# Sliding-window attention feeding a gated feed-forward block: transposes of queries and keys on TensorE in place of DMA, and a later place for the softmax sums

## Chip, cores and metric

The kernel runs on one core of one Trainium2 chip. The metric is the device time of one execution in microseconds (us). A core has TensorE (PE, matmuls into PSUM), VectorE (DVE), ScalarE (ACT), GpSimd (POOL) and SyncE (SP), which run side by side and wait for each other by semaphores; SP, ACT and POOL also issue DMA transfers, which 16 DMA engines carry out.

## What is computed

Attention with 8 batches, 8 heads, 576 positions and head size 64. Each query sees itself and the 127 positions before it; the score is lowered by a slope per head times the distance. Then a gated feed-forward block on all 4608 tokens (512 wide, 1536 hidden).

```python
scores = scale * np.matmul(q, k.transpose(0, 1, 3, 2))
mask = (rel >= 0) & (rel < window)                  # window = 128
scores = np.where(mask, scores + bias[None], -1000000000.0)
attn = np.exp(scores - max);  attn = attn / (sum(attn) + 1e-09)
attn_out = np.matmul(attn, v)                        # (8, 8, 576, 64)
x = attn_out.transpose(0, 2, 1, 3).reshape(4608, 512)
out = (gelu(x @ w_gate) * (x @ w_val)) @ w_out       # (4608, 512)
```

## The kernel before, in words

The feed-forward block works through nine groups g of 512 tokens, the attention through eight batches b of 576 tokens; results of the attention go into a ring `xT` (features on partitions, 3072 tokens), from which the groups read. The order of all engines is the order in which the program is written; nothing is rescheduled. While group g is worked on, batches g+1 and g+2 of the attention are slipped in between (line 915, `steps`, and the loop from line 933).

**A group.** `gate_val(g, f)` (line 615) runs for f = 0 to 11: eight matmuls of 512 columns (four with `wg`, four with `wv`, line 632), then Gelu on ACT (line 639) and a multiplication on DVE (line 640) into `hid`. `out_part(g, n)` (line 662) does n of the group's 16 output parts, three matmuls each (line 669); every fourth part is copied from PSUM by DVE or ACT (line 674, chosen by `by_dve`, line 651) and later stored by an SP DMA (`store`, line 657, called ahead of the next parts).

**A batch.** Queries and keys are loaded by POOL DMAs, cast to bf16, into `qs` and `ks` (token rows on partitions; two buffers, by b % 2), v into `vb`. `transposes_dma` (line 173) has SP issue six DMA transposes per batch that write `qT` and `kT` with the head dimension on partitions. Batches 0 and 1 have transposes of their own on TensorE (lines 784, 797 and 154). Scores are 64x64-weight matmuls: `scores` (line 235, batches 1 and 2) or `scores2` (line 267, from batch 3). Exponentials run on ACT (line 229), the decay with distance is multiplied in by DVE (line 232).

In `scores2` and in `products` two halves of the array write one PSUM bank, so the second half must come after the first: `relay` (line 208) puts a no-op on another engine's queue, SP by default, which waits for the first half's last matmul and on which the second half's first matmul waits.

**Sums from batch 3 on.** `add` (line 378) folds the overlapping blocks of probabilities into `T` (DVE, lines 385 to 394). `sums4` (line 426) sums `T` over partitions with 32 small matmuls (line 437) and takes reciprocals on DVE (line 442). `gather` (line 446) writes them to a DRAM buffer `rd` with two DMAs from ACT's queue, `spread_dma` (line 454) reads them back with two DMAs, repeated over 64 partitions each, into `rb`. `values` (line 547) runs the products with v (line 501) and multiplies them by `rb` into `xT` (DVE, line 565).

The written order for groups 2 to 5, b = g+2: gate steps f = 0 to 11, with the sums of batch b-1 after f = 3 (4 in group 2), its gather after 5 (6) and its spread after 7 (8); then 4 output parts, products of batch b-1, 4 parts, first scores of b and its additions, 4 parts, second scores of b and its additions, 4 parts. `load_qk(g+3)` and `load_v(g+2)` are issued by POOL at f = 9, behind a small copy (`mark`) that waits for that gate step. The DMA transposes of batch g+2 are issued at the start of group g.

Group g+1 reads the last 512 - 64(g+1) of its tokens from batch g+1, so its first gate matmuls need the scaled products of that batch.

`bank()` hands out PSUM banks, eight in all; a bank is free again when its last reader has run.

Of the kernel before, what the change touches and what calls it, by code (L numbers as in the profile page):

```python
# [8 lines left out]
BF16 = mybir.dt.bfloat16  # L9
# [23 lines left out]
def kernel(  # L33
# [10 lines left out]
    nc = tc.nc  # L44
    B, H, S, D = q.shape
# [22 lines left out]
    def bank():  # L68
        return psum.tile([128, 512], FP32, name="ps")
# [11 lines left out]
    ident = consts.tile([128, 128], BF16, name="ident")  # L81
# [11 lines left out]
    mark = consts.tile([1, 2], BF16, name="mark")  # L93
    last = consts.tile([128, DM], FP32, name="last")
# [7 lines left out]
    def rows(j):  # L102
        return 64 if j == 4 else 128
# [12 lines left out]
    def load_qk(b):  # L116
        load(qs[b % 2], q, b)
        load(ks[b % 2], k, b)

    def load_v(b, js=range(5)):  # L120
        load(vb[b % 2], v, b, js, 64)
# [48 lines left out]
        for n, lo in ((0, 0), (1, 384)):  # L170
            untangle(copy, b, n, what, c, c + 1, ps[:, lo:576])

    def transposes_dma(b):
        def of_k():
            nc.sync.dma_start_transpose(
                out=kT[b % 2].rearrange("p c (j t) -> p (c j) t", t=128),
                in_=ks[b % 2].rearrange("p j x -> p (j x)"))

        if b > 3:
            of_k()  # L180
        for j in range(5):
            nc.sync.dma_start_transpose(
                out=qT[b % 2][:, :, 128 * j:128 * j + 128], in_=qs[b % 2][:, j, :])
        if b <= 3:
            of_k()


    Ps = [consts.tile([128, H, 896], BF16, name=f"P{i}") for i in range(2)]
# [4 lines left out]


    def keys(b, c, m):
        if b < 2:
            return kT[b][:, c, 64 * m:64 * m + 64]
        at = 512 * (m // 2) + 128 * c + 64 * (m % 2)
        return kT[b % 2].rearrange("p c x -> p (c x)")[:, at:at + 64]

# [7 lines left out]
    def relay(mm, engine=nc.sync):  # L208
        by = engine.nop()
        depends(by, mm)  # L210
        return by
# [52 lines left out]

    def scores2(b, c0):
# [24 lines left out]
        todo.sort(key=lambda t: t[0])  # L292
        count, by = {c: 0 for c in pairs}, {}
        total = sum(len(parts_of(x, True)) for x in (0, 1))
        for _, i, c, both, x, m, q0, w, col in todo:
            half = slice(64 * i, 64 * i + 64)
            ps, col = (shared[c], col + 256 * i) if both else (own[c, i], col)
            mm = nc.tensor.matmul(  # L298
                out=ps[64 * x:64 * x + 64, col:col + w], lhsT=keys(b, c, m)[half, :],
                rhs=qT[b % 2][half, c, q0:q0 + w], start=True, stop=True)  # L300
            if both and i == 0:
                count[c] += 1
                if count[c] == total:
                    by[c] = relay(mm)
# [92 lines left out]
    sumrow, recip = {}, {}  # L397
# [45 lines left out]

    flat = {}

    def gather(b):
        flat[b] = d_pool.tile([H, S], FP32, name="rd")
        for s in (0, 1):
            lo, w = shape(b, s)
            nc.scalar.dma_start(  # L450
                out=flat[b][:, lo:lo + 2 * w].rearrange("h (x t) -> x h t", x=2),
                in_=sumrow[b][0:128:8, lo:lo + w])

    def spread_dma(b):
        for i in (0, 1):
            nc.scalar.dma_start(
                out=recip[b][64 * i:64 * i + 64, :, :],
                in_=flat[b][i:H:2, :].unsqueeze(0).to_broadcast((64, 4, S)))

# [153 lines left out]
    hid = {}  # L613
# [34 lines left out]
    acc = {}  # L648


    by_dve = {0: (0,), 1: (0, 1)}

# [245 lines left out]

    nc.gpsimd.memset(T[64:128, :, 0:64], 0.0)
    nc.gpsimd.memset(Ps[1][:, :, 0:64], 0.0)
    for t in (qs[0], ks[0]):
        nc.gpsimd.memset(t[64:128, 4, :], 0.0)
    load_qk(2)


    acts = (act, act, act, act)
    scales = []
    todo = {  # L910
        0: [("table",), ("s", 1, 0, (0, 1)), ("o", 0, 0, 0), ("o", 0, 1, 0), ("s", 1, 0, (2, 3)), ("o", 0, 0, 1), ("s", 1, 1, (0, 1)), ("o", 0, 1, 1), ("s", 1, 1, (2, 3), masks), ("pv+", 1, 0), 4, ("transposes", 2), ("pv+", 1, 1), 4],
        1: [("table",), ("s", 2, 0, (0, 1)), 3, ("s", 2, 0, (2, 3)), 2, ("s", 2, 1, (0, 1)), 2, ("s", 2, 1, (2, 3), masks), ("pv+", 2, 0, scales), 1, ("scale",), 2, ("pv+", 2, 1), 1, 2, ("s2", 3, 0), ("add", 3, 0), 3, ("s2", 3, 2), ("add", 3, 2, None, (0,))],
    }

    def steps(g):
        b = g + 2
        if g in todo:
            return todo[g]
        if b > B:
            return [16] if g < NG - 1 else [12, ("last", g)]  # L920
        if b == B:
            return [4, ("pv", b - 1), 12]
        return [("table",), 4, ("pv", b - 1), 4, ("s2", b, 0), ("add", b, 0), 4, ("s2", b, 2),
                ("add", b, 2), 4]


    def exp_table():
        nc.scalar.preload_act_table_set("natural_log_exp_and_others")

    RUN = {"s": scores, "s2": scores2, "add": add, "sum4": sums4, "gather": gather, "spread": spread_dma, "pv": values, "pv+": values_and_sums,  # L930
           "masks": flush, "table": exp_table, "transposes": transposes_dma, "last": out_last, "scale": lambda: scales.pop()(), "o": out_half}

    for g in range(NG):
        if 1 <= g < B - 2:
            transposes_dma(3 if g == 1 else g + 2)
        if g == 1:

            nc.gpsimd.tensor_copy(out=mark, in_=kT[1][0:1, 0, 512:514])
            load_qk(4)
            load_v(3)  # L940
        for f in range(9 if g == 0 else 0, NF):
            gate_val(g, f)
            if g == 2 and f == 2:
                add(3, 2, act, (1,))
            if g == 0 and f == 10:
                masks_of_last_blocks(0, 8)
            if g == 0 and f == 9:
                for c in range(4):
                    for w in (0, 1):
                        transpose(1, w, c, (act, dve)[w])  # L950
            if 2 <= g < B - 1:
                if f == (4 if g == 2 else 3):
                    sums4(g + 1)
                if f == (6 if g == 2 else 5):
                    gather(g + 1)
                if f == (8 if g == 2 else 7):
                    spread_dma(g + 1)
                if f == 9 and g + 2 < B:

                    nc.gpsimd.tensor_copy(out=mark, in_=hid[g][0:1, f, 0:2])  # L960
                    if g + 3 < B:
                        load_qk(g + 3)
                    load_v(g + 2)
        if g == 0:
            nc.gpsimd.memset(Ps[0][:, :, 0:64], 0.0)
            for t in (qs[1], ks[1]):
                nc.gpsimd.memset(t[64:128, 4, :], 0.0)
        for item in steps(g):
            if isinstance(item, int):
                out_part(g, item)  # L970
            else:
                RUN[item[0]](*item[1:])
        store()
        if g == 0:

            nc.gpsimd.tensor_copy(out=mark, in_=qT[0][0:1, 0, 512:514])
            load_qk(3)
            load_v(2)

# [29 lines left out]
```

## Time and profile before

| | |
|---|---|
| median of 3 runs | 338.54 us (338.36 to 339.22) |
| the profiled execution | 337.69 us |
| its span, first to last instruction | 335.9 us |
| TensorE granted clock | 1.000 |
| line 632, gate and value matmuls, PE busy | 223.4 us |
| line 669, output matmuls, PE busy | 87.6 us |
| line 501, products and some sums | 5% of the chain that ended last |
| DMA transposes | 36 issued by SP (30 of queries, 6 of keys) |

A row of the profile page's groups gives line, engine, operation, `out<-in` by the program's names, shapes and count, then busy time, mean nanoseconds of one instruction, and how long the engine was idle ahead of it and on what. Matmuls are pipelined, so the mean of one (379 ns for 512 columns) is longer than the distance between two starts. The chain of work that ended last is followed back from the last instruction: what it names is what the end was waiting for. Times inside the profile count from the start of the span.

### The profile page before, as it was taken

What the parts mean: (1) busy time and instruction counts of PE and PEld (TensorE: products, weight loads), DVE (VectorE), ACT (ScalarE), POOL (GpSimd) and SP (SyncE); (2) the same over time, 40 slices, a digit from 0 to 9 for tenths busy, and PEclk for the clock granted to TensorE, in tenths of its full rate; (3) what the DMA queues carried; (4) which work ended last, traced back from release to release, by engine and by line L of the source; (5) the groups of instructions that cost most, each with busy time, mean ns of one, the idle gap of its engine ahead of it and who ended that gap; (6) DMA issues with size and microseconds to landing.
All of it is one profiled execution on the core that took longest, in us unless ns stands there. A gap on an engine that the chain in (4) does not pass through costs nothing.

```text
span 335.9 us, 8087 instructions
## 1 busy us (share of the span) xinstructions
PE 327.7 (98%) x3273; PEld 169.5 (50%) x3316; DVE 192.9 (57%) x356; ACT 170.3 (51%) x318; POOL 108.3 (32%) x144
## 2 busy tenths in 40 slices
PE   8999999999999999999999999999999999999996
PEld 6667556444554454445544554445444544444444
DVE  7888776445779458845693469546964324303320
ACT  8974687438796339332943275335732233223322
POOL 6974784481193293009400860050000000000000
PEclk9999999999999999999999999999999999999999
DMA  8999999999999899969975999394105110020002
GB/s 216 170 197 191 205 164 189 117 181 137 183 161 153 181 184 198 164 161 134 184 163 104 153 187 179 81 166 83 64 3 140 64 65 0 1 96 31 0 31 96
DMA packets 149914, 43.49 MB, mean 129 GB/s; under 512 B 133588, under 2 KB 142836, under 8 KB 149876
## 3 DMA queue, kind: packets, MB, share of 16 engines
q0 software_dynamic: 107456, 18.10, 70.5%
q1 hardware_dynamic: 39104, 18.62, 25.4%
q10 hardware_dynamic: 3316, 6.25, 7.8%
q8 instruction: 26, 0.43, 0.5%
q14 instruction: 12, 0.10, 0.1%
HBM read 43.65 MB, written 9.53 MB: 158 GB/s over the span
## 4 chain that ended last, share of the span: by engine, by line
PE 94%; issue 2%; DMA 1%; DVE 1%; ACT 1%; SPq 0%; DVEq 0%
PE ps L632 56%; PE ps L669 25%; PE ps L501 5%; PE ps L298 2%; PE ps L689 2%; PE ps L216 1%; DMA qs<-in_q_dram 1%; PE ps L437 1%; PE ps L705 1%; PE ps L154 1%; ACT P L229 0%; SPq L726 0%; DVE xT L537 0%; DVE qT L162 0%; ACT rb L583 0%
## 5 line engine op out<-in xcount | busy, mean ns | idle before, releaser
L640 DVE TENSOR_TENSOR hT<-ps,gelu 128x512 bf16<-128x512 f32 (+3 forms) x117 | 73.6, 645 | 92.6 <-PE ps L632 86.0
L639 ACT ACTIVATE gelu<-ps 128x512 bf16<-128x512 f32 (+3 forms) x117 | 65.0, 564 | 101.7 <-PE ps L632 98.3
L632 PE MATMUL ps<-xT,wv 128*128 128x512 bf16 (+4 forms) x468 | 112.2, 361 | 0.4
L632 PE MATMUL ps<-xT,wg 128*128 128x512 bf16 (+4 forms) x456 | 111.2, 361 | 0.7
L669 PE MATMUL ps<-wo,hT 128*128 128x512 bf16 x375 | 87.6, 379 | 2.1 <-issue 1.4
L632 PEld LDWEIGHTS <-wv 128*128 128x128 bf16 x472 | 45.1, 98 | 48.6
L632 PEld LDWEIGHTS <-wg 128*128 128x128 bf16 x472 | 44.4, 98 | 47.6
L669 PEld LDWEIGHTS <-hT 128*128 128x128 bf16 x396 | 37.0, 98 | 43.4 <-issue 0.3
L229 ACT ACTIVATE P<-ps 128x512 bf16<-128x512 f32 (+1 forms) x108 | 51.3, 581 | 2.0 <-PE ps L216 1.5
L674 ACT COPY osb<-ps 128x512 f32<-128x512 f32 x27 | 15.9, 588 | 50.8 <-PE ps L669 50.8
L232 DVE TENSOR_TENSOR P<-P,emask 128x768 bf16<-128x768 bf16 x60 | 31.2, 555 | 18.2 <-ACT P L229 16.4
L112 POOL DMA_DIRECT2D vb<-in_v_dram x40 | 33.9, 886 | 6.5 <-DMA qs<-in_q_dram 2.3
L112 POOL DMA_DIRECT2D qs<-in_q_dram x30 | 25.2, 858 | 2.3 <-issue 1.8
L112 POOL DMA_DIRECT2D ks<-in_k_dram x30 | 25.4, 894 | 0.1
L960 POOL COPY mark<-hT 1x2 bf16<-1x2 bf16 x4 | 0.7, 174 | 75.7 <-DVE hT L640 75.7
L501 PE MATMUL ps<-P,vb 64*64 64x192 bf16 (+2 forms) x752 | 17.4, 220 | 0.4 <-issue 0.2
L565 DVE TENSOR_TENSOR xT<-ps,rb 128x512 bf16<-128x512 f32 (+3 forms) x34 | 14.6, 501 | 4.6 <-PE ps L501 4.6
L501 PEld LDWEIGHTS <-vb 64*64 64x64 bf16 x752 | 14.8, 107 | 3.6 <-issue 2.8
L385 DVE TENSOR_TENSOR T<-P 64x1024 bf16<-64x1024 bf16 x20 | 13.7, 686 | 0.6
L442 DVE RECIPROCAL r<-ps 128x128 f32<-128x128 f32 (+1 forms) x10 | 9.8, 1019 | 0.0
L298 PEld LDWEIGHTS <-kT 64*64 64x64 bf16 x440 | 7.5, 107 | 4.4 <-issue 4.4
L639 ACT ACT_TABLE_LOAD x7 | 9.0, 1283 | 1.3 <-PE ps L632 1.3
(93 smaller groups left out, 186.4 us busy)
## 6 DMA issues: line engine op xcount, KB each, us to landing
out_dram<-osb SPq DMA_DIRECT2D x35, 256.0 KB
rb<-rd ACTq DMA_DIRECT2D x10, 576.0 KB
vb<-in_v_dram POOLq DMA_DIRECT2D x32, 128.0 KB, 6.5
qs<-in_q_dram POOLq DMA_DIRECT2D x24, 128.0 KB, 5.5
ks<-in_k_dram POOLq DMA_DIRECT2D x24, 128.0 KB, 7.0
wo<-in_moe_w_out_dram POOLq DMA_DIRECT2D x4, 384.0 KB, 12.0
wg<-in_moe_w_gate_dram POOLq DMA_DIRECT2D x5, 256.0 KB, 8.5
wv<-in_moe_w_val_dram POOLq DMA_DIRECT2D x5, 256.0 KB, 9.3
```

The lines of the kernel that those rows point to most:

```text
L112: nc.gpsimd.dma_start(out=t[at:at + n, j, :].rearrange("p (h d) -> p h d", h=H), in_=src[b][:, 128 * j:128 * j + n, :].rearrange("h p d -> ...
L229: nc.scalar.activation(out=dst, in_=src, func=AF.Exp, scale=0.125)
L232: nc.vector.tensor_tensor(out=dst, in0=dst, in1=m, op=ALU.mult)
L298: mm = nc.tensor.matmul(out=ps[64 * x:64 * x + 64, col:col + w], lhsT=keys(b, c, m)[half, :], rhs=qT[b % 2][half, c, q0:q0 + w], start=Tru ...
L385: nc.vector.tensor_tensor(out=to[half, :, x:x + 7:2], in0=P[half, :, 0:10:3], in1=P[half, :, 1:11:3], op=ALU.add)
L501: mm = nc.tensor.matmul(out=out, lhsT=lhsT, rhs=prob(b)[half, c, i, col:col + q1 - q0], start=all(t[2] != u for t in todo[:n]), stop=True, ...
L565: nc.vector.tensor_tensor(out=xT[:, c, at:at + e - a], in0=src, in1=recip[b][:, c, a:e], op=ALU.mult)
L632: nc.tensor.matmul(out=ps[:, a:e], lhsT=w[:, c, 128 * f:128 * (f + 1)], rhs=xT[:, c, t0 + lo + a:t0 + lo + e], start=begins and a == 0, st ...
L639: nc.scalar.activation(out=gl[:, 0:n], in_=pg, func=AF.Gelu)
L640: nc.vector.tensor_tensor(out=hid[g][:, f, lo:hi], in0=pv, in1=gl[:, 0:n], op=ALU.mult)
L669: nc.tensor.matmul(out=acc[g], lhsT=hid[g][:, f, 128 * t:128 * (t + 1)], rhs=wo[:, f, :], start=(f == 0), stop=(f == NF - 1))
L674: (nc.vector.tensor_copy if g < B - 2 and t in by_dve.get(g, (0,)) else nc.scalar.copy)(out=osb, in_=acc[g])
```

## The change

- The DMA transposes are gone. `transposes(b, c)` transposes head pair c of queries and keys of batch b on TensorE: five transposes each into one PSUM bank, then one copy (queries on ACT, keys on DVE unless given). For batches 4 to 7 they run in group b-2 after gate steps 6 and 8, two pairs each; for batch 2 in group 1 after steps 5 and 7; for batch 3 in group 1 after step 11 (pairs 0 and 1) and among the output parts (pairs 2 and 3, one at a time, both copies on DVE). `kT` now has the same layout for all batches.
- For batches 3 to 6 the sums move behind the first 4 output parts, just ahead of the first scores of batch b; gather and spread follow those scores, on SP's queue in place of ACT's; the products with v move behind the second scores and 4 more parts. The second scores' relays go to POOL. The additions of batches 4 to 7 move into the gate steps of the next group. For batch 7 the sums stay among the gate steps, two later.
- `load_qk` is issued at f = 6, `load_v` behind the second scores, after a marker that waits for the spread. Four memsets of the last rows of `qs` and `ks` and two markers are gone. All output copies of groups 2 to 5 are on ACT.

```diff
-    def transposes_dma(b):
-        def of_k():
-            nc.sync.dma_start_transpose(
-                out=kT[b % 2].rearrange("p c (j t) -> p (c j) t", t=128),
-                in_=ks[b % 2].rearrange("p j x -> p (j x)"))
...
-        for j in range(5):
-            nc.sync.dma_start_transpose(
-                out=qT[b % 2][:, :, 128 * j:128 * j + 128], in_=qs[b % 2][:, j, :])
...
+    def transposes(b, c, copies=None):
+        for w, (src, dst, copy) in enumerate(zip((qs, ks), (qT, kT), copies or (act, dve))):
+            ps = bank().bitcast(BF16)
+            for j in range(5):
+                n = rows(j)
+                nc.tensor.transpose(
+                    out=ps[:, 128 * j:128 * j + n], in_=src[b % 2][0:n, j, 128 * c:128 * c + 128],
+                    identity=ident[0:n, 0:n])
+            copy(out=dst[b % 2][:, c, 0:S], in_=ps[:, 0:S])
...
-    def gather(b):
+    def gather(b, queue=nc.scalar):
...
-    def spread_dma(b):
+    def spread_dma(b, queue=nc.scalar):
...
-    by_dve = {0: (0,), 1: (0, 1)}
+    by_dve = {0: (0,), 1: (0, 1), 2: (), 3: (), 4: (), 5: ()}
...
-        return [("table",), 4, ("pv", b - 1), 4, ("s2", b, 0), ("add", b, 0), 4, ("s2", b, 2),
-                ("add", b, 2), 4]
+        return [("table",), 4, ("sum4", b - 1), ("s2", b, 0), ("gather", b - 1, nc.sync),
+                ("spread", b - 1, nc.sync), 4, ("s2", b, 2, nc.gpsimd), ("load v", b), 4, ("pv", b - 1), 4]
+
+    def load_v_behind(b):
+        nc.gpsimd.tensor_copy(out=mark, in_=recip[b - 1][0:1, 0, S - 1:S].bitcast(BF16))
+        load_v(b)
...
+            if g == 1 and f in (5, 7):
+                transposes(2, f - 5)
+                transposes(2, f - 4)
+            if g == 1 and f == 11:
+                transposes(3, 0)
+                transposes(3, 1)
+                nc.gpsimd.tensor_copy(out=mark, in_=hid[g][0:1, f, 0:2])
+                load_qk(4)
+                load_v(3)
+            if 2 <= g < B - 2 and f in (6, 8):
+                transposes(g + 2, f - 6)
+                transposes(g + 2, f - 5)
...
-            if 2 <= g < B - 1:
-                if f == (4 if g == 2 else 3):
+            if 3 <= g < B - 1:
+                turns = (0, 1, 2, 3) if g == B - 2 else (1, 2, 4, 5)
+                if f in turns:
+                    n = turns.index(f)
+                    add(g + 1, n // 2 * 2, None, (n % 2,))
+            if g == B - 2:
+                if f == 5:
                     sums4(g + 1)
-                if f == (6 if g == 2 else 5):
+                if f == 7:
                     gather(g + 1)
-                if f == (8 if g == 2 else 7):
+                if f == 9:
                     spread_dma(g + 1)
-                if f == 9 and g + 2 < B:
-
-                    nc.gpsimd.tensor_copy(out=mark, in_=hid[g][0:1, f, 0:2])
-                    if g + 3 < B:
-                        load_qk(g + 3)
-                    load_v(g + 2)
+            if 2 <= g < B - 3 and f == 6:
+
+                nc.gpsimd.tensor_copy(out=mark, in_=hid[g][0:1, f, 0:2])
+                load_qk(g + 3)
```

More of the change, by code (lines that the diff above doesn't have):

```diff
@@ L171, in transpose @@
             untangle(copy, b, n, what, c, c + 1, ps[:, lo:576])
-    def transposes_dma(b):
-        def of_k():
-            nc.sync.dma_start_transpose(
-                out=kT[b % 2].rearrange("p c (j t) -> p (c j) t", t=128),
-                in_=ks[b % 2].rearrange("p j x -> p (j x)"))
-        if b > 3:
-            of_k()
-        for j in range(5):
-            nc.sync.dma_start_transpose(
-                out=qT[b % 2][:, :, 128 * j:128 * j + 128], in_=qs[b % 2][:, j, :])
-        if b <= 3:
-            of_k()
+    def transposes(b, c, copies=None):
[7 more added lines that the diff above has]
+            copy(out=dst[b % 2][:, c, 0:S], in_=ps[:, 0:S])
     Ps = [consts.tile([128, H, 896], BF16, name=f"P{i}") for i in range(2)]
@@ L195, in keys @@
     def keys(b, c, m):
[L196 to L199, printed above, removed]
+        return kT[b % 2][:, c, 64 * m:64 * m + 64]
     def depends(use, on):
@@ L263, in parts_of, with scores2 @@
         return ((4 + x, 384 + 64 * x, 64, 0), *last)
-    def scores2(b, c0):
+    def scores2(b, c0, engine=nc.sync):
         pairs = (c0, c0 + 1)
@@ L303, in scores2 @@
                 if count[c] == total:
-                    by[c] = relay(mm)
+                    by[c] = relay(mm, engine)
             if both and i and c in by:
@@ L449, in gather @@
             lo, w = shape(b, s)
-            nc.scalar.dma_start(
+            queue.dma_start(
                 out=flat[b][:, lo:lo + 2 * w].rearrange("h (x t) -> x h t", x=2),
                 in_=sumrow[b][0:128:8, lo:lo + w])
-    def spread_dma(b):
+    def spread_dma(b, queue=nc.scalar):
         for i in (0, 1):
-            nc.scalar.dma_start(
+            queue.dma_start(
                 out=recip[b][64 * i:64 * i + 64, :, :],
@@ L902 @@
     nc.gpsimd.memset(Ps[1][:, :, 0:64], 0.0)
-    for t in (qs[0], ks[0]):
-        nc.gpsimd.memset(t[64:128, 4, :], 0.0)
     load_qk(2)
@@ L910 @@
     todo = {
-        0: [("table",), ("s", 1, 0, (0, 1)), ("o", 0, 0, 0), ("o", 0, 1, 0), ("s", 1, 0, (2, 3)), ("o", 0, 0, 1), ("s", 1, 1, (0, 1)), ("o", 0, 1, 1), ("s", 1, 1, (2, 3), masks), ("pv+", 1, 0), 4, ("transposes", 2), ("pv+", 1, 1), 4],
-        1: [("table",), ("s", 2, 0, (0, 1)), 3, ("s", 2, 0, (2, 3)), 2, ("s", 2, 1, (0, 1)), 2, ("s", 2, 1, (2, 3), masks), ("pv+", 2, 0, scales), 1, ("scale",), 2, ("pv+", 2, 1), 1, 2, ("s2", 3, 0), ("add", 3, 0), 3, ("s2", 3, 2), ("add", 3, 2, None, (0,))],
+        0: [("table",), ("s", 1, 0, (0, 1)), ("o", 0, 0, 0), ("o", 0, 1, 0), ("s", 1, 0, (2, 3)), ("o", 0, 0, 1), ("s", 1, 1, (0, 1)), ("o", 0, 1, 1), ("s", 1, 1, (2, 3), masks), ("pv+", 1, 0), 4, ("pv+", 1, 1), 4],
+        1: [("table",), ("s", 2, 0, (0, 1)), 3, ("transposes", 3, 2, (dve, dve)), ("s", 2, 0, (2, 3)), 2, ("transposes", 3, 3, (dve, dve)), ("s", 2, 1, (0, 1)), 2, ("s", 2, 1, (2, 3), masks), ("pv+", 2, 0, scales), 1, ("scale",), 2, ("pv+", 2, 1), 1, 2, ("s2", 3, 0), ("add", 3, 0), 3, ("s2", 3, 2), ("add", 3, 2, None, (0,))],
     }
@@ L922, in steps @@
             return [4, ("pv", b - 1), 12]
-        return [("table",), 4, ("pv", b - 1), 4, ("s2", b, 0), ("add", b, 0), 4, ("s2", b, 2),
-                ("add", b, 2), 4]
+        return [("table",), 4, ("sum4", b - 1), ("s2", b, 0), ("gather", b - 1, nc.sync),
[3 more added lines that the diff above has]
+        load_v(b)
     def exp_table():
         nc.scalar.preload_act_table_set("natural_log_exp_and_others")
-    RUN = {"s": scores, "s2": scores2, "add": add, "sum4": sums4, "gather": gather, "spread": spread_dma, "pv": values, "pv+": values_and_sums,
-           "masks": flush, "table": exp_table, "transposes": transposes_dma, "last": out_last, "scale": lambda: scales.pop()(), "o": out_half}
+    RUN = {"s": scores, "s2": scores2, "add": add, "sum4": sums4, "gather": gather, "spread": spread_dma, "pv": values, "load v": load_v_behind, "pv+": values_and_sums,
+           "masks": flush, "table": exp_table, "transposes": transposes, "last": out_last, "scale": lambda: scales.pop()(), "o": out_half}
     for g in range(NG):
[L934 to L940, printed above, removed]
         for f in range(9 if g == 0 else 0, NF):
             gate_val(g, f)
+            if g == 1 and f in (5, 7):
[10 more added lines that the diff above has]
+                transposes(g + 2, f - 5)
             if g == 2 and f == 2:
@@ L950 @@
                         transpose(1, w, c, (act, dve)[w])
-            if 2 <= g < B - 1:
-                if f == (4 if g == 2 else 3):
+            if 3 <= g < B - 1:
[5 more added lines that the diff above has]
+                if f == 5:
                     sums4(g + 1)
-                if f == (6 if g == 2 else 5):
+                if f == 7:
                     gather(g + 1)
-                if f == (8 if g == 2 else 7):
+                if f == 9:
                     spread_dma(g + 1)
-                if f == 9 and g + 2 < B:
-                    nc.gpsimd.tensor_copy(out=mark, in_=hid[g][0:1, f, 0:2])
-                    if g + 3 < B:
-                        load_qk(g + 3)
-                    load_v(g + 2)
+            if 2 <= g < B - 3 and f == 6:
+                nc.gpsimd.tensor_copy(out=mark, in_=hid[g][0:1, f, 0:2])
+                load_qk(g + 3)
         if g == 0:
             nc.gpsimd.memset(Ps[0][:, :, 0:64], 0.0)
-            for t in (qs[1], ks[1]):
-                nc.gpsimd.memset(t[64:128, 4, :], 0.0)
         for item in steps(g):
@@ L974 @@
         if g == 0:
-            nc.gpsimd.tensor_copy(out=mark, in_=qT[0][0:1, 0, 512:514])
             load_qk(3)
```

## Prediction

> **What bounds the kernel now.** I read the page's busy table first, then the chain of work that ended last.
>
> ```profile
> span 335.9 us, 8087 instructions
> ...
> PE 327.7 (98%) x3273; PEld 169.5 (50%) x3316; DVE 192.9 (57%) x356; ACT 170.3 (51%) x318; POOL 108.3 (32%) x144
> ...
> PE 94%; issue 2%; DMA 1%; DVE 1%; ACT 1%; SPq 0%; DVEq 0%
> ```
>
> See that TensorE is busy 98% of the span and carries 94% of the chain; DMA, where the transposes now run, carries 1%. "Busy" can hide pauses between pipelined matmuls, so I next read the chain in order of time over one group (columns: start us, us, what).
>
> ```profile
> 131.50 6.91 PE ps L632 x32
> 138.41 0.61 PE ps L437 x32
> ...
> 155.53 1.53 PE ps L501 x76
> 157.22 2.54 PE ps L669 x11
> 159.75 0.80 PE ps L298 x33
> ...
> 163.25 0.80 PE ps L298 x33
> ...
> 166.75 6.91 PE ps L632 x32
> ```
>
> See that 32 gate matmuls take 6.91 us, 0.216 us each, and that one group lasts 166.75 - 131.50 = 35.25 us. Its 96 gate and 48 output matmuls need 144 x 0.2159 = 31.1, its sums 0.6, products 1.6 and two score sets 1.6: 34.9 us. About 0.35 us is left, over ten changes of kind, 0.04 each. The group has no hole.
>
> Third, the timeline of SP and PE in this group: are the DMA transposes late for anyone?
>
> ```profile
> 132.78 4.41 SPq L175 DMA_TRANSPOSE kT<-ks  x1
> 137.24 7.60 SPq L182 DMA_TRANSPOSE qT<-qs  x5
> ```
>
> They are issued by 144.84, and the scores that read them start at 159.75. In the list of waits PE never waits for them; the longest waits on them are two POOL markers (12.7 and 9.0 us). So what is removed ends nothing.
>
> **Part 1, the transposes: +13.9 us on PE.** Each of six batches gets 4 head pairs x 2 x 5 = 40 transposes, 32 of 128 columns and 8 of 64. The nearest rows with full 128x128 weights and 128 columns:
>
> ```profile
> 30.15 0.39 PE L632 MATMUL ps<-xT,wg 128*128 128x128 bf16 x4
> 30.38 0.39 PE L632 MATMUL ps<-xT,wv 128*128 128x128 bf16 x4
> 30.60 0.39 PE L632 MATMUL ps<-xT,wg 128*128 128x128 bf16 x4
> ```
>
> 0.39 is the modelled busy time; the pitch is the difference of starts, 0.223 per four, 55.8 ns each, a new weight load for each included. The existing transposes of line 784 agree: 6 in 0.34 us on the chain (57 ns). A 64-column one: half the stream, 29 ns. Per batch 32 x 55.8 + 8 x 29 = 2.02 us, and six are 12.1 us. Bursts: 13 (two per batch, one more for batch 3), each a change of kind in and out. Such a change costs 0.04 by the group above and 0.1 by the transposes of batch 1 (last gate matmul streams until 35.45, line 154 starts at 35.55). I take 0.07: 26 x 0.07 = 1.8. Together 13.9, between 12.1 and 14.7.
>
> The Trainium skill, "TensorE: Matmul & The Clock Gate", Part 4, speaks against the change: it gives about 275 ns for a 128x128 transpose in a kernel and says that transposes do not keep the clock up. 240 of them would be 66 us by that. This trace has 57 ns at a granted clock of 1.000, so the rule is not used. For the change, "VectorE: DVE Perf Modes", "The three transpose paths", has 390 ns on TensorE against 1309 ns by DMA; that compares two durations, and here the slower path was hidden.
>
> The 48 copies out of PSUM (128x576) have no row. ScalarE lies between 0.59 (128x512) and 0.51 + 0.36 = 0.87 (384 and 192 apart), VectorE between 0.69 and 0.55 + 0.35 = 0.90; I take 0.65 and 0.75, by the slope between the 192 and 384 rows. A burst gives each engine two: 1.3 and 1.5 us. Beside a gate step (1.73 us of PE, 0.60 on ACT, 0.69 on DVE) the burst itself adds 1.1 us of PE, so the work fits. From group 3 the added sums (2 x 2.7 us by lines 385 to 394) sit in the gate loop too: DVE then needs 7 x 0.69 + 5.4 + 1.5 = 11.7 us up to the first burst, where PE takes 13.2. Cost nothing, with PE as cover and eight banks as slack; without it, up to 0.7 us a burst (rival 2).
>
> **Part 2, sums later: +8.5 us.** For batches 3 to 6 the sums move from the fourth or fifth gate step to just before the next batch's scores, and the way from sums to scaled products is now short of time. Its legs, from the last group, where little else uses the DMA engines:
>
> ```profile
> 244.87 1.96 DVE L442 RECIPROCAL r<-ps 128x128 f32<-128x128 f32 x2
> 262.43 2.88 DVE L565 TENSOR_TENSOR xT<-ps,rb 128x512 bf16<-128x512 f32 x6 [2.94 <-PE ps L501]
> ```
> ```profile
> 247.51 1.10 ACTq L450 DMA_DIRECT2D rd<-r  x2
> 251.09 1.30 ACTq L456 DMA_DIRECT2D rb<-rd  x2
> ```
>
> Time 0 is the end of the sums. The reciprocals take 0.15 to 2.1. The second gather is issued at 2.2; before, it was issued at 248.05 and that queue's bytes ended at 249.7, so with a little for the receipt 1.9: landed 4.1. The spread waits for it; issued at 251.09 its bytes ended at 258.0, so 6.9: landed at 11.1. Before, all of this hid behind seven gate steps and more. Then DVE scales four head pairs, 0.68 each (line 565, 128x512): the last is ready at 11.2 + 2.7 + 0.1 = 14.0.
>
> PE meanwhile has scores and 4 output parts (159.75 to 163.25, 3.50), the same again, then products and 4 parts (155.53 to 159.75, 4.22): 11.22 us. Then the next group's first gate matmuls read all four head pairs of these tokens (batch g+1 begins inside group g+1), the fourth one at 11.22 + 0.65 = 11.87. PE waits 14.0 - 11.9 = 2.1 us, four times (groups 3 to 6): 8.5. The ends: with the shortest legs (1.67 and 6.7) 1.7 us, with the longest (2.8 for the gather of 177 us, 7.3 for the spread of 112 us, both beside DMA transposes that are now gone) 3.5. So 6.8 to 14.
>
> Queued behind the new waits: on SP, behind the spread's wait, the second output store and the relays of the products (line 209). The spread is issued by 5.6 and the products start at 7.0, so the relays are free with 1.4 us to spare. On POOL the relays of the second scores stand before the v marker, and q/k loads end long before; the v loads wait for the spread, then have half a group. Four output copies go from DVE (0.69) to ACT (0.59), which has room. Removed memsets and markers only free POOL.
>
> **Part 3, the rest: +0.5 us.** In group 1's steps DVE gets four copies (3.0 us) among its masks; the masks that the products of batch 2 need end about 1.4 us ahead of them now, and PE also gets later. In group 6 the sums at step 5 follow additions that end about 0.7 us after PE asks. Between 0 and 2; I take 0.5. Start, groups 7 and 8 and the tail stay.
>
> **Sum.** 13.9 + 8.5 + 0.5 = 22.9. The profiled execution took 337.69 us (span 335.9 and 1.8 around it): 360.6. The median of the runs is 338.54, 0.85 above: 361.4. I say 361.
>
> **Rivals.**
> 1. *The sums stay covered.* PE's 11.9 us suffice if the spread lands by 9.0 after the sums, 2.1 earlier than by the rows, or if something on PE stretches there. For it: DMA transposes no longer share the engines with gather and spread. Against: the legs are from a stretch without them. Time: 338.5 + 13.9 + 0.5 = 353, from 350 with the lowest transposes to 355.
> 2. *New waits on PSUM or SP.* If copies, additions and masks on DVE, or the relays behind the spread, hold PE 0.7 us per burst (13) or 2 us more per group (4), another 8 to 9 us: 370, 367 to 375. Against: DVE is 57% busy.
> 3. *The transposes run beside other matmuls.* This is the one that ends faster. The half-array transposes of line 154 do pair up: 80 in 2.17 us, 27 ns each. If full ones hid likewise under gate matmuls and the sums stayed covered, the group would lose only its wait: PE idles 0.91 us of the 38.9 in group 1, so 338.5 - 0.9 = 337.6 or a little more. It decides below about 4 ns per transpose. Against: line 784's use the whole array at 57 ns. Nor did DMA transposes slow PE: 49 gate matmuls take 10.74 us both at 139.40, beside them, and at 306.35, without.
>
> **Chances.** Forecast 0.55 (356 to 367), rival 1 0.27, rival 2 0.13, rival 3 0.05. The range holds forecast and rival 1 and the low edge of rival 2: 349 to 368. About 0.3% is what a measurement of this kernel can tell from no change: faster 0.03, same 0.02, both from rival 3; slower 0.95.
>
> **What would show it.** Right: 240 more matmuls on PE in bursts of 20 taking 1.0 to 1.2 us; PE waiting about 2 us for DVE's scaling (line 565) at the starts of groups 3 to 6, and nowhere else in the middle; steady groups of about 39.7 us instead of 35.25. Wrong: groups of about 37.6 us (rival 1); PE waiting for the copies or an SP relay (rival 2); transposes at a pitch far from 56 ns either way.

## The result, and the profile after

The changed kernel takes **378.03 us** (median of four runs, 376.40 to 378.83), the kernel before 338.68 on the same chip: a ratio of **1.115** (95% interval 1.111 to 1.120), 39.35 us slower. The forecast was 361, with a range to 368. The direction held, the size did not: about 17 us of loss were not foreseen. The profiled execution took 377.76 us against 337.69, so the traces have 40.1 us to explain.

The profile page of the changed kernel: the span, the engines' busy time, two rows of the 40 slices, and the shares of the chain that ended last.

```profile
span 376.0 us, 8536 instructions
...
PE 357.5 (95%) x3508; PEld 186.1 (49%) x3556; DVE 200.6 (53%) x378; ACT 187.7 (50%) x344; POOL 106.2 (28%) x142
...
PE   8999999999999997999899997999989999999996
...
PEclk9999999999999998999999998999989999999999
...
PE 80%; DMA 11%; DVE 5%; issue 1%; SPq 1%; ACT 1%; DVEq 0%
```

TensorE's share of the chain fell from 94 to 80%. DMA and DVE, which stood at 1% each, now carry 11 and 5%: something is waited for that was covered. The PE row has dents of one digit, and the clock row, whose profile before had a granted clock of 1.000, dips in three slices. The chain in order of time over one group (start us, us, what) names all of it but the clock:

```profile
201.68 1.74 PE ps L178 x20
...
214.70 1.89 PE ps L662 x8
216.59 0.64 PE ps L430 x32
...
217.26 1.98 DVE r L435 x2
...
219.26 1.74 DMA rd<-r
...
221.12 0.63 SPq L449
...
221.79 7.45 DMA rb<-rd
...
229.37 2.36 DVE xT L558 x7
...
231.76 9.59 PE ps L625 x36
```

Read it in three steps. A burst of 20 transposes (line 178; 178, 625, 662, 430, 435, 449 and 558 here are the lines of the transposes, gate matmuls, output matmuls, sums, reciprocals, spread and scaling) takes 1.74 us on the chain. After the sums (216.59) the path leaves PE for reciprocals, gather, spread and scaling, and returns only at 231.76. Then 36 gate matmuls take 9.59 us, 0.266 each; before the change 32 took 6.91, 0.216 each. In time that is not a wait at all, PE is busy. The windows of this kernel show why (columns: window, busy time and count of PE, PEld, DVE, ACT and POOL, granted TensorE clock, DMA share, GB/s):

```profile
229.00:232.00 3.00, 1.38 (x4) 0.41 (x5) 2.63 (x8) 1.87 (x2) 2.58 (x4) 0.96 1.71 233
232.00:236.00 4.00, 4.00 (x12) 1.47 (x11) 1.20 (x4) 1.03 (x2) 0.00 (x0) 0.61 1.52 151
236.00:241.00 5.00, 5.00 (x25) 2.27 (x24) 4.39 (x9) 1.61 (x4) 0.00 (x0) 1.00 0.00 0
```

PE is busy throughout the second window and yet starts 12 matmuls in 4 us, against 25 in 5 us in the third. The granted clock is 0.61. The same happens behind the waits of groups 3 and 6, at 0.65 and 0.57; in group 4 the clock stays at 1.00, and 36 gate matmuls take 7.93 us instead of 9.30, 9.59 and 9.62.

Put together, from the profiled execution:

| | forecast | measured |
|---|---|---|
| transposes: 11 bursts of 20 at 1.84 us, 2 of 10 at 0.92 | 13.9 | 22.1 |
| waits for scaling, groups 3 to 6: 3.5, 2.45, 2.8, 3.2 | 8.5 | 12.0 |
| TensorE at a lowered clock behind three of the waits | none | 4.7 |
| the rest | 0.5 | 1.3 |
| sum | 22.9 | 40.1 |

The burst is measured from its first transpose to the next gate matmul (201.51 to 203.35). A wait is the start of the fourth gate matmul less the time at which it was due, by the pitch of the matmuls ahead of it. The clock's 4.7 us are the three excesses over 7.93. The rest is the remainder: 0.5 us of it lie ahead of the gate matmuls of group 1, 0.7 behind the first of group 8.

### The profile page after: what moved, and what is told of

Same layout as the page of the kernel before. It is cut to its first block, busy times and chain, and to the rows that moved or that the text cites. A ratio compares the mean times of both kernels' runs of the same rounds, so it can differ in the third digit from the quotient of the medians.

```text
span 376.0 us, 8536 instructions
## 1 busy us (share of the span) xinstructions
PE 357.5 (95%) x3508; PEld 186.1 (49%) x3556; DVE 200.6 (53%) x378; ACT 187.7 (50%) x344; POOL 106.2 (28%) x142
## 4 chain that ended last, share of the span: by engine, by line
PE 80%; DMA 11%; DVE 5%; issue 1%; SPq 1%; ACT 1%; DVEq 0%
PE ps L625 51%; PE ps L662 14%; DMA rb<-rd 8%; PE ps L178 6%; PE ps L494 3%; DVE xT L558 2%; DVE r L435 2%; DMA rd<-r 2%; PE ps L209 1%; PE ps L682 1%; DMA wo<-in_q_dram 1%; PE ps L430 1%; SPq L449 1%; PE ps L698 1%; PE ps L154 1%
## 5 line engine op out<-in xcount | busy, mean ns | idle before, releaser
L633 DVE TENSOR_TENSOR hT<-ps,gelu 128x512 bf16<-128x512 f32 (+3 forms) x117 | 75.0, 648 | 103.4 <-PE ps L625 98.3
L625 PE MATMUL ps<-xT,wg 128*128 128x512 bf16 (+4 forms) x463 | 116.7, 367 | 9.8 <-DVE xT L558 9.1
L625 PE MATMUL ps<-xT,wv 128*128 128x512 bf16 (+4 forms) x460 | 113.9, 368 | 0.4
L667 ACT COPY osb<-ps 128x512 f32<-128x512 f32 x31 | 18.2, 587 | 55.1 <-PE ps L662 31.1
L181 ACT COPY qT<-ps 128x576 bf16<-128x576 bf16 x22 | 14.0, 638 | 10.0 <-PE ps L178 10.0
```

The costliest lines, as they stand in the source:

```text
L625: nc.tensor.matmul(out=ps[:, a:e], lhsT=w[:, c, 128 * f:128 * (f + 1)], rhs=xT[:, c, t0 + lo + a:t0 + lo + e], start=begins and a == 0, st ...
L633: nc.vector.tensor_tensor(out=hid[g][:, f, lo:hi], in0=pv, in1=gl[:, 0:n], op=ALU.mult)
L667: (nc.vector.tensor_copy if g < B - 2 and t in by_dve.get(g, (0,)) else nc.scalar.copy)(out=osb, in_=acc[g])
```

## The experiments

The theory after the result had three parts: the transposes cost more because of the 64-row ones among them; the waits are longer because the spread lands later than its last bytes; and the short pauses lower the clock. Its rivals were that one of the two halves of the change held the whole surprise, that the additional loss was contention between the halves, and that the pauses' length alone explained what came behind them. All times below are medians, each with its ratio to the kernel before on the same chip.

### The halves apart

**TensorE transposes, everything else of the sums in the old place.**

```diff
-        return [("table",), 4, ("sum4", b - 1), ("s2", b, 0), ("gather", b - 1, nc.sync),
-                ("spread", b - 1, nc.sync), 4, ("s2", b, 2, nc.gpsimd), ("load v", b), 4, ("pv", b - 1), 4]
+        return [("table",), 4, ("pv", b - 1), 4, ("s2", b, 0), ("add", b, 0), 4, ("s2", b, 2),
+                ("add", b, 2), 4]
...
+                if f == (4 if g == 2 else 3):
+                    sums4(g + 1)
...
```

> TensorE transposes as in the changed kernel, but sums, gather, spread, additions, products and v loads placed and queued as before the change. Theory (the later sums cost stalls of 2.4 to 3.4 us at four group starts and lower clocks behind them, about 17 us; the transposes cost 22 us by themselves): 338.7 + 22 = 361 us, no PE wait for the scaling, clock 1.000. Rival (the waits at the group starts come from the copies and additions that crowd DVE and PSUM): the waits stay, 370 us or more.

Measured: 362.01, 1.069 [1.066, 1.071], 23.4 us over before. The clock was 0.999, and PE no longer waited for the scaling at the starts of groups 3 to 6. (Three waits of 0.2 to 0.3 us for it are left, in the scores of group 2.)

**DMA transposes, the changed order of sums, gather, spread and products.**

```diff
-            if 2 <= g < B - 2 and f in (6, 8):
-                transposes(g + 2, f - 6)
-                transposes(g + 2, f - 5)
+        if 1 <= g < B - 2:
+            transposes_dma(3 if g == 1 else g + 2)
```

> The other half: DMA transposes as before the change, but sums, gather, spread, additions, products, load_qk and v loads placed and queued as in the changed kernel. Theory: 338.7 + 17 = 355 to 356 us, PE waits for the scaling at the starts of groups 3 to 6 and has a granted clock below 1 for some 4 us behind most of them. Rival (the waits need the TensorE transposes): 338 to 344 us.

Measured: 355.45, 1.049 [1.045, 1.054], 16.8 us over before. The clock fell behind three of the four waits again (0.60, 0.62 and 0.57), with not one transpose on TensorE in these groups.

23.4 and 16.8 are 40.2, and both together cost 39.35. So the halves add up; neither is the cause of the other's loss.

### Why a burst takes 1.84 us

One burst of the changed kernel, in the timeline of PE (start us, busy us, line, output and inputs, weights, columns, count):

```profile
201.51 0.39 PE L178 MATMUL ps<-ident,qs 128*128 128x128 bf16 x4
...
201.83 0.20 PE L178 MATMUL ps<-ident,qs 64*128 64x64 bf16 x1
201.96 0.23 PE L178 MATMUL ps<-ident,ks 128*128 128x128 bf16 x1
```

Four full transposes start at 201.51, .57, .62 and .68. The one of 64 rows should follow at 201.73 and starts at 201.83; the next full one starts 0.13 later, not 0.03. A five takes 0.45 us instead of the 0.25 that its columns ask for. To see whether the 64 columns or the change of form costs this, one kernel does away with the form, and one keeps every 64-row transpose but puts them together.

**Every transpose with 128 rows** (the last 64 hold zeros and the copies leave them out).

```diff
-                n = rows(j)
+                n = 128
...
+    for t in (qs[0], ks[0]):
+        nc.gpsimd.memset(t[64:128, 4, :], 0.0)
...
```

> The changed kernel, but the fifth transpose of each five takes all 128 rows of its block (rows 64 to 127 zeroed beforehand by four memsets on POOL, as before the change) and writes 128 columns, of which 64 are used. In the changed kernel four 128-row transposes start 0.055 us apart, but the 64-row one and the one after it start 0.28 us apart together. Theory (the switch of the array between 128 and 64 rows costs 0.18 us per five): a five takes 0.28 us in place of 0.46, a burst of 20 about 1.2 in place of 1.84; 48 fives x 0.18 = 8.6 us less, about 369.5 us. Rival (transposes of token rows are slow whatever their shape, by their weight loads): a fifth full one costs as much, no change, about 378 us.

Measured: 367.53, 1.085 [1.080, 1.089]. The timeline of a burst in this kernel:

```profile
195.91 0.44 PE L178 MATMUL ps<-ident,qs 128*128 128x128 bf16 x5
196.19 0.44 PE L178 MATMUL ps<-ident,ks 128*128 128x128 bf16 x5
...
197.02 0.38 PE L625 MATMUL ps<-xT,wg 128*128 128x512 bf16 x1
```

20 transposes in 1.11 us, 55.6 ns each, from the gate matmul before to the gate matmul behind. More columns are less time. Of the 11.0 us between the two profiled executions 8.3 are the bursts and 2.4 the clock, which fell behind two waits in place of three. And there is nothing left for a change between matmuls and transposes: of one form, they follow each other without a gap.

**The four 64-row transposes of a burst together, behind the sixteen full ones.**

```diff
...
+        for js in (range(4), (4,)):
+            for c, src, dst, copy, ps in todo:
+                for j in js:
...
```

> The changed kernel, but within a burst all 128-row transposes come first and the four 64-row ones last, in a row. The same 20 instructions, one change to 64 rows and back per burst in place of four. Theory (the change of rows costs): a burst saves 3 x 0.18 = 0.5 us, 11 bursts and two half ones give about 6 us less, 372 us. Rival (a 64-row transpose costs 0.2 us by itself): no change, 378 us.

Measured: 367.92, 1.089 [1.086, 1.091]. The end of a burst:

```profile
196.45 0.39 PE L179 MATMUL ps<-ident,ks 128*128 128x128 bf16 x4
196.76 0.20 PE L179 MATMUL ps<-ident,qs 64*128 64x64 bf16 x1
196.81 0.19 PE L179 MATMUL ps<-ident,ks 64*128 64x64 bf16 x1
196.83 0.19 PE L179 MATMUL ps<-ident,qs 64*128 64x64 bf16 x1
196.86 0.19 PE L179 MATMUL ps<-ident,ks 64*128 64x64 bf16 x1
```

Among themselves the 64-row ones start 0.02 to 0.05 apart, which is what the forecast had for them. The burst takes 1.21 us (195.78 to 196.99) with one pair of changes, 1.84 with four: about 0.2 us for each pair. The 13 bursts together are 7.3 us shorter. That the kernel came in some 4 us below its expectation has mostly another cause: in its profile the clock fell behind none of the four waits, and in its six executions the granted clock was 0.990 to 0.999, against 0.985 in the changed kernel.

**Full tiles and the sums in the old place**, both edits above in one kernel.

```diff
-                n = rows(j)
+                n = 128
...
-        return [("table",), 4, ("sum4", b - 1), ("s2", b, 0), ("gather", b - 1, nc.sync),
-                ("spread", b - 1, nc.sync), 4, ("s2", b, 2, nc.gpsimd), ("load v", b), 4, ("pv", b - 1), 4]
+        return [("table",), 4, ("pv", b - 1), 4, ("s2", b, 0), ("add", b, 0), 4, ("s2", b, 2),
+                ("add", b, 2), 4]
...
```

> TensorE transposes with full 128-row tiles, sums placed as before the change: the cheapest form of the first half alone. Theory: 338.6 + 12 bursts' worth of 1.22 us (14.6) = 353 to 354 us, the clock at 1.000. Rival (TensorE transposes can be hidden once nothing else waits): under 345 us; a version that beats the kernel before is not expected.

Measured: 354.43, 1.045 [1.043, 1.047], 15.3 us over before. Transposes at 55.6 ns are 13.3 of these (240 times 55.6). Of the other 2.0, 0.8 are the small waits in the scores of group 2; the rest was not traced. Without change of form, the transposes cost about what the forecast put down for them, 13.9, but that is in part luck: its 13.9 hold 1.8 us for changes of kind that the gate matmuls and full transposes do not show, and price the 64-row ones at half.

### Whether the clock is a cost of its own

**36 matmuls of zeros ahead of the first gate step of groups 3 to 6**, into a bank nobody reads. They fill the pause and do nothing for the chain that PE waits for.

```diff
+            if f == 0 and 3 <= g <= 6:
+                keep_busy(bank(), 36, 128)
```

> The changed kernel with 36 matmuls of zeros (128 columns, 2.0 us) into a spare bank ahead of the first gate step of groups 3 to 6, where PE waits; they end before the last head pair is scaled, so the wait itself ends as late as before. Theory (the clock falls because PE pauses): the granted clock stays at 1.000 behind the four waits, and the 1.5 to 1.9 us that gate matmuls at half speed cost at three of them go: about 5 us less, 373 us. Rival (the clock falls for another reason, say what runs beside it): clock as in the changed kernel, 378 us or, if the fill is in the way, more.

Measured: 372.95, 1.101 [1.098, 1.103]. The timeline of the filler and then two of the windows, with the same columns as above:

```profile
143.68 2.17 PE L74 MATMUL ps<-zeros 128*128 128x128 bf16 x36
...
145.50:149.50 4.00, 3.29 (x19) 1.44 (x18) 2.97 (x7) 2.36 (x3) 1.49 (x2) 1.00 2.01 187
230.00:234.00 4.00, 3.66 (x17) 1.66 (x17) 2.36 (x7) 1.50 (x3) 0.14 (x1) 1.00 1.77 168
```

The clock stays at 1.00 behind all four waits, and the median is 5.1 us lower. By the measure of the table above the waits are 10.8 us together, 1.2 less than in the changed kernel, and the 36 gate matmuls behind each take as long as those of group 4 in the changed kernel, so the 4.7 us of the table are gone whole. So work that computes nothing made the kernel faster, and the term of 4.7 us is the clock's. The Trainium skill, "TensorE: Matmul & The Clock Gate", section "Why this matters for your kernels", asks for no idle gaps of PE above some 3 us between bursts of matmuls. The pauses here are shorter: 2.2, 1.1, 1.3 and 1.9 us, each with three of 0.2 to 0.3 behind it, and three of the four lowered the clock. By that rule none would have.

Which ones do can be read off the traces. In the middle of a kernel a lowered stretch always lasts 3.41 us, at a granted clock of 0.50, and the starts of the lowered stretches of one trace are whole multiples of 3.41 us apart: in the changed kernel 146.41, 231.74 and 276.11, 25 and 13 multiples. So I divided each trace into pieces of 3.41 us on its own grid. The piece ahead of each of the changed kernel's four long runs of gate matmuls and the piece behind it (columns as above, with PE's matmuls as the first count):

```profile
143.00:146.41 3.41, 0.81 (x3) 0.21 (x3) 1.93 (x4) 1.38 (x2) 3.41 (x5) 1.00 1.50 279
146.41:149.82 3.41, 3.39 (x8) 1.09 (x8) 1.32 (x4) 1.08 (x2) 0.20 (x1) 0.50 1.97 187
187.37:190.78 3.41, 1.85 (x7) 0.65 (x8) 2.88 (x6) 2.16 (x3) 2.27 (x3) 1.00 1.91 226
190.78:194.20 3.42, 3.42 (x18) 1.53 (x17) 1.74 (x3) 1.16 (x3) 0.00 (x0) 1.00 1.40 149
228.33:231.74 3.41, 1.25 (x4) 0.30 (x4) 2.38 (x8) 1.81 (x2) 3.25 (x4) 1.00 1.53 268
231.74:235.15 3.41, 3.39 (x9) 1.19 (x9) 1.46 (x4) 0.65 (x2) 0.00 (x0) 0.50 1.89 184
272.70:276.11 3.41, 1.77 (x6) 0.59 (x7) 2.88 (x6) 2.08 (x3) 2.54 (x4) 1.00 1.80 236
276.11:279.52 3.41, 3.41 (x9) 1.21 (x8) 2.17 (x4) 0.97 (x2) 0.00 (x0) 0.50 1.51 162
```

Busy times are modelled, so I counted how long the matmuls of a piece stream, 0.42 ns per column from their starts (0.216 us for 512): 0.43, 1.35, 0.65 and 1.28 us. In the twelve traces of this document all 11 drops behind a wait follow a piece with 0.43 to 1.34 us of streaming, and past the first microseconds, where the clock has yet to rise, every piece with so little is followed by one and no piece with 1.35 us or more is. So a pause lowers the clock here when it leaves less than some 1.35 us of work in one piece, and pauses that a border parts can be longer: with stores held to the group's end (below), a pause of 1.17 us, nearly all of it in one piece with its three followers, left 1.34 us there and lowered the clock; one of 1.73 us, cut off from its followers by a border, left 1.66 and 2.13 and did not. This is read off the traces; no run moved a pause against the grid.

### Why the spread takes 8.3 us

The forecast took 6.9 us from issue to landing. In the changed kernel the four spreads took 8.7, 8.0, 8.1 and 8.4, mean 8.3. Output stores are issued on the same queue right behind; the question was whether they hold it up.

**Stores held back to the group's end.**

```diff
...
-                ("spread", b - 1, nc.sync), 4, ("s2", b, 2, nc.gpsimd), ("load v", b), 4, ("pv", b - 1), 4]
+                ("spread", b - 1, nc.sync), ("hold", 1), 4, ("s2", b, 2, nc.gpsimd), ("load v", b), 4, ("pv", b - 1), 4, ("hold", 0)]
...
```

> The changed kernel, but in groups 2 to 5 the output stores that stood behind the spread on SP's queue are held until the group's end (four output buffers in place of three). Theory (their bytes share the DMA engines with the spread, which took 7.3 to 8.0 us from issue in place of the 6.7 to 7.0 of before): each of the four waits gets about 1.2 us shorter, 5 us less by that and perhaps a clock drop or two less: 370 to 373 us. Rival (the spread is as fast as it can be; the stores lie behind it): 378 us.

Measured: 373.72, 1.103 [1.100, 1.106]; spreads 7.7 to 8.2 us. Not decisive: SP, which waits for nothing else there, issued the held stores some 4 us after the spread (225.18 after 220.96), still beside it. Between the profiled executions 3.0 us are gained: 1.4 by shorter waits, 1.3 by the clock, which fell two times in place of three.

**Stores held until the next group's first gate step has run**, by a no-op on SP that waits for it.

```diff
+            if hold and f == 0:
+                relay(mm)
+                hold.clear()
+                store()
```

> Like the run with stores held, but the stores of groups 2 to 5 wait, by a no-op on SP, for the first gate step of the next group, so that none of their bytes can run beside the spread (in the run before, SP issued them as soon as the relays of the products were through, 4 us after the spread, and the spread took 7.85 us from its first issue, after 8.3 in the changed kernel). Theory (the spread was mis-sized only by the stores beside it): 6.9 to 7.0 us, as beside nothing in the kernel before: each wait 1.3 us shorter than in the changed kernel, 370 to 372 us with the clock drops that stay. Rival (the spread on SP's queue takes 7.8 us even alone, its landing is seen later than its last bytes): as the run with stores held, 373 to 375 us.

Measured: 373.77, 1.102 [1.098, 1.105]: the rival's number. With no store beside them the spreads still take 7.8, 8.0, 7.8 and 8.25 us. The chain in this kernel:

```profile
219.01 0.63 SPq L449
...
219.68 7.13 DMA rb<-rd
...
226.93 2.36 DVE xT L558 x7
```

The first issue is at 219.01, the waiter sees the landing at 226.81 (219.68 + 7.13), and by the trace's DMA records the spread's last packet ends at 226.14. So 0.7 us lie between the last bytes and the moment at which DVE may go on; in the eight spreads of this kernel and the changed one it is 0.67 to 0.84. The mean of the four spreads, 8.0 against 8.3, puts the stores at 0.3 us. The forecast had read its 6.9 us off a transfer's bytes. That leaves 0.3 to 0.4 us of the 8.3 open: even with no store beside them the bytes take 7.1 to 7.5 us here. Of the 4.3 us that the kernel gains, 3.0 are the clock, which in this profile fell behind one wait only.

### Whether an earlier place cures the waits

**Sums, gather and spread ahead of the first four output parts, not behind them.** The relays of the first scores go to POOL, so that they do not stand behind the spread on SP's queue.

```diff
-        return [("table",), 4, ("sum4", b - 1), ("s2", b, 0), ("gather", b - 1, nc.sync),
-                ("spread", b - 1, nc.sync), 4, ("s2", b, 2, nc.gpsimd), ("load v", b), 4, ("pv", b - 1), 4]
+        return [("table",), ("sum4", b - 1), ("gather", b - 1, nc.sync), ("spread", b - 1, nc.sync), 4,
+                ("s2", b, 0, nc.gpsimd), 4, ("s2", b, 2, nc.gpsimd), ("load v", b), 4, ("pv", b - 1), 4]
```

> The changed kernel, but the sums, with gather and spread behind them on SP, stand ahead of the first four output parts in place of behind them; the relays of the first scores go to POOL, so that they don't stand behind the spread's wait. PE has 2.64 us more of work between the sums and the next group's first gate step. Theory (what is short is cover between sums and scaling, by 2.4 to 3.4 us): the waits shrink to 0 to 0.8 us, and the clock stays up: 338.6 + 22 + 1 to 3 = 362 to 364 us. Rival (the scaling is late for another reason, as DVE's or SP's order): 370 us or more.

Measured: 362.86, 1.071 [1.068, 1.074]. The row of PE's waits for the scaling (us in total, times, longest), in the changed kernel and then in this one:

```profile
PE ps L625 <- DVE xT L558: 9.1, 15, 2.2
```
```profile
PE ps L625 <- DVE xT L558: 1.0, 5, 0.2
```

(The list counts idle time between modelled ends, which is less than the delay of starts in the table above.) Four output parts are 12 matmuls, 2.6 us; moved by that, the four waits fall from 12.0 to 2.4 us by the table's measure and all of the clock's drops are gone, 15.2 us for a change of order. The products may stay where the change put them.

**The same order with DMA transposes**: what is left of the change if both losses are taken out.

> DMA transposes as before the change, the changed kernel's order, but with the sums, gather and spread ahead of the first four output parts (2.64 us more cover). Theory (the later sums cost nothing but their four waits and the clock drops behind them): with waits of 0 to 0.8 us, 339 to 342 us, at the kernel before or just above it. Rival (the order costs something else too, queues or banks): 346 us or more.

Measured: 343.46, 1.014 [1.009, 1.020]: between the two expectations, and some 1.5 us above the first. From fourth gate matmul to fourth gate matmul, groups 3 to 5 last 36.0, 36.3 and 35.5 us against 35.25 before the change, but group 2 lasts 37.6 against 35.0. Its chain:

```profile
118.59 1.89 DVE r L442 x2
...
120.50 3.84 DMA rd<-r
...
125.11 7.36 DMA rb<-rd
```

The gather takes 3.84 us here, with loads and DMA transposes beside it, where it takes 1.74 in the changed kernel's chain above, and the reciprocals begin late because a gate multiplication stands before them on DVE. In the cover of this chain PE also stands still for 1.35 us, up to 122.66: the first scores now come so early that the DMA transposes of the queries are not done. So the transposes, which ended nothing before the change, do hold PE in this order. That would explain the miss; it was not tried by itself.

None of these kernels beats the kernel before. The one nearest to it has undone the transposes and moved the sums back part of the way.

## Why the prediction was wrong in size and right in direction

**What bounds the kernel: right.** TensorE without holes, DMA transposes off the path. The first half alone, which takes them away, gains nothing back: 23.4 us of loss against 22.1 of transposes.

**Part 1, the transposes, +13.9: the term that failed most (22.1, +8.2).** The pitch of full ones was right, 55.6 against 55.8 ns. The failing step is "A 64-column one: half the stream, 29 ns". The stream is that short (0.02 to 0.05 us, where four stand together), but each lone 64-row transpose between full ones changes the form of the array, and back, and the pair costs 0.2 us: 48 fives are some 9.6 us. The rows for 128 columns all had one form, and the kernel before has no 64-row transpose between full ones. But the forecast knew changes of kind of 0.04 to 0.1 us, and counted them only at the two ends of a burst; at 0.1 each the 96 inside the bursts give the 9.6. The Trainium skill, "TensorEngine Tiling (Array Packing)", section "Key Properties", says that changing the tiling mode drains TensorE; it bore on this step and I did not weigh it. The runs fit it and add the 0.2 us, for which it has no figure; that it is a drain, no run shows. The second term, 0.07 us for a change of kind, was wrong in the other direction: the full-tile kernel has none between gate matmuls and transposes. The copies were no cost, as forecast: 0.638 us on ACT against 0.65, and 0.456 on DVE, far below the 0.75 put down.

**Part 2, later sums, +8.5: the mechanism right, one leg mis-sized (12.0, +3.5).** The waits stand at the starts of groups 3 to 6 and end with the scaling, as forecast. Reciprocals (1.98) and gather (1.74) were as forecast or sooner. The failing leg is "issued at 251.09 its bytes ended at 258.0, so 6.9": a wait ends when the landing is seen, some 0.7 us after the bytes, the stores add some 0.3, and 0.3 to 0.4 stay open. The gather's leg had "a little for the receipt", the spread's had nothing.

**What the forecast did not have: the clock, 4.7 us.** It priced each wait at its own length. It took the granted clock of 1.000 as given, while the change put pauses where there had been none.

**Part 3, +0.5: small, as forecast.** What is left over is 1.3 us, group 1 costs nothing beyond its transposes, and PE's one wait for a relay on SP is 0.23 us.

**The rivals.** That the sums stay covered fell: they are uncovered by more than forecast. New waits on PSUM or SP, 370 us, came nearer to the time than the forecast, but by chance: PE's list of waits has none of them above that 0.23 us. Transposes beside other matmuls fell: the full ones take the array at 55.6 ns each, and 240 of them show up in the total. The range ended at 368 because no case let two terms be too small at once, or had a term for the clock.

**What stays open.** The length of a pause does not decide whether the clock falls: with stores held to the group's end, pauses of 1.17 and 1.32 us did it, 1.73 and 0.98 did not; in the grouped kernel 1.51 to 1.86 did not in the profiled execution. The grid of 3.41 us sorts all of them, but no run tested it, and where the grid lies cannot be planned from these runs: with DMA transposes and late sums, two executions had a granted clock of 0.985 and took 356.5 us, two had 0.995 and took 353.7 and 354.4. So part of the loss is luck of the execution.

## What to carry to other kernels

Price an instruction with its neighbours: a short matmul of another tile shape between full ones costs the change of form twice, and padding it to the full shape can be cheaper. Where a chain through DMA loses its cover, take each leg up to the moment at which the waiter goes on, not up to the last bytes. And on a TensorE that never paused, a new pause of 1 to 2 us costs its length and, behind 11 of the 24 such pauses in these traces, 1.0 to 1.7 us more in clock; give the chain a few parts of matmuls more ahead, or fill the pause.

## What of the hardware was not expected

- The pair of changes between transposes of 128 and of 64 rows takes 0.2 us; between matmuls of 512 columns and full 128x128 transposes there is none.
- A pause of 1.0 to 2.2 us, with shorter ones behind it, can halve TensorE's rate for 3.41 us: a pitch of 0.43 us in place of 0.216, at a granted clock of 0.50. In these traces it does so when less than some 1.35 us of streaming are left in one piece of a grid of 3.41 us. Matmuls of zeros in the pause avert it.
- Transposes count as work for the clock: in the profiles of the grouped kernel and three others one piece near 35 us holds the 80 transposes of line 154 of the kernel before (2.2 us) and only 1.1 to 1.2 us of other matmuls, and the clock stays at 1.00.
- Some 0.7 us (0.67 to 0.84) pass between a spread's last bytes and the end of the wait for it.
